# Attention and a bilinear feed-forward on one core: the second pair of heads transposed ahead of its turn, and denominators moved directly behind the weighted values

## The chip, the cores and the metric

The kernel runs on one core of a Trainium2 chip. The metric is the device time of one execution in microseconds; less is better. The core's engines are named as in the profile: PE is the matrix engine (PEld its weight loads, which can run beside its matmuls), DVE the vector engine, ACT the scalar engine, POOL the GpSimd engine, SP the engine that only issues transfers here.

## The reference

Two parts are chained. The first is attention with routing: every query and every key is given to the nearest of 16 centroids, and a query sees only the keys of its own centroid. The second is a feed-forward with two input matrices whose results are multiplied.

```python
# q, k, v: (4 batches, 8 heads, 768 positions, 64); centroids: (8, 16, 64)
q_assign = argmax(q_n @ c_n.T);  k_assign = argmax(k_n @ c_n.T)      # q_n, k_n, c_n: normalised rows
mask   = q_assign[..., :, None] == k_assign[..., None, :]
scores = where(mask, (q @ k.T) / 8, -1e9)
attn   = exp(scores - max);  attn = attn / (sum(attn) + 1e-9)
x      = (attn @ v) laid out as (3072 tokens, 512)
out    = ((x @ w_a) * (x @ w_b)) @ w_out             # w_a, w_b: 512 x 1536, w_out: 1536 x 512
```

## The kernel before

Two heads form a pair, so there are 16 pairs `p`; four pairs make a batch. The main loop counts groups `g`; six groups belong to a pair (`l` is the place in the pair), and a group is two blocks of 128 keys against 384 queries, for both heads. A group scores its own blocks (a one-hot product that carries the mask, then the product of queries and keys), and weighs the values with the exponentials of the group before. Every third group closes a half pair with its denominators: a product of a matrix of ones with the last exponentials and with a running sum `acc`. Between these lie the preparation of the next pair (`ready[l]`) and pieces of the feed-forward (`ffn`).

```python
def prep_transpose(p, i):                  # 4 of the 12 transposes of pair p, into one PSUM bank
    ps = ps_m.tile([P, 512], FP32, name="m")             # ps_m: three banks in turn
    for n in range(4):
        w, j = divmod(4 * i + n, NJ)
        nc.tensor.transpose(out=ps[:, n*P:(n+1)*P], in_=qks[p][:, w, j]..., identity=ident)
    dst = qkTs[p][:, i * 512:(i + 1) * 512]
    if p == 0 and i != 1: nc.vector.tensor_copy(out=dst, in_=ps)
    else:                 nc.scalar.copy(out=dst, in_=ps)

def prep_sim(p):    # similarity with the centroids: 4 matmuls over qkTs[p], 32 columns each
def prep_assign(ps, quarters): # five DVE steps: maximum, >=, times rank, maximum, ==
def prep_onehot_first(kq):     # pair 0: six bf16 transposes on PE, one copy on ACT, one on DVE
def keep_busy(n):   # n transposes of the identity into a bank that nobody reads

# prep_steps(p), pairs 1 to 3:
return [both(lambda: prep_transpose(p, 0), lambda: prep_transpose(p, 1)),
        both(lambda: prep_sim(p), lambda: load_v(p)),
        lambda: todo.extend(prep_assign(prep_across(p))), lambda: None,
        lambda: prep_onehot(p, 1), lambda: None]
# pairs 4 to 15: the transposes are DVE stream transposes in 32x32 blocks (across), prep_sim in step 1

# ... start of the program (cut)
first = load_first()          # q and k of pair 0: q from SP's queue, k from ACT's
centroids_in()                # norms of the centroids on DVE and ACT
order_first(*first, 0, nc.vector.tensor_copy); order_first(*first, 1, nc.scalar.copy)
# ...
keep_busy(18)
prep_transpose(0, 0); centroids_across(); prep_transpose(0, 1); prep_transpose(0, 2)
# ...
load(1); load_v(0); load_w(0); load_w(1)
prep_sim(0); keep_busy(3)
across = prep_across(0)
rest_of_first = score((0, 1))              # the q.k part of the first two blocks
keep_busy(4)
for kq in range(2):
    for step in prep_assign(across, kq): step()
    prep_onehot_first(kq)
    if kq == 0:
        keep_busy(5); rest_of_first(); keep_busy(7)
for g in range(NG + 3):
    # ...
    if 0 < g < NG: score(now)
    check_inverses()
    if 0 < g <= NG:
        for u in before: add_up(u)         # acc += exponentials, on DVE (later on POOL too)
    flush_w()
    if 0 < g <= NG: weigh(before)
    if g < NG: ready[l]()
    late = int(g > EARLY)                  # EARLY = 25
    if g % 3 == late and 0 < g - late:
        denominators(*divmod(g // 3 - 1, 2))
    # ... weights, feed-forward pieces (cut)
    if l == 0 and p + 1 < NPAIR:
        if not by_blocks(p + 1): prep_transpose(p + 1, 2)      # by_blocks: p >= 4
        load(p + 2)
```

Of the kernel before, what the change touches and what calls it, by code (L numbers as in the profile page):

```python
# [8 lines left out]
FP32 = mybir.dt.float32  # L9
# [21 lines left out]
P = 128  # L31
# [105 lines left out]
def short_path(nc, tc, ctx, c, cn, centroids_in, casts, n_far, q, k, v,  # L137
# [3 lines left out]
    B, H, S, D = q.shape  # L141
    NC = 16
    DM, DF = moe_w_a.shape
    NJ = S // P
# [6 lines left out]
    def pool(name, bufs, space=None):  # L151
        kw = {} if space is None else {"space": space}
        return ctx.enter_context(tc.tile_pool(name=name, bufs=bufs, **kw))

    zero = pool("zero", 1)
    qkp = pool("qkp", 1)
# [8 lines left out]
    hp_ = pool("hp", 2)  # L165
# [9 lines left out]
    ident, identb, ones, rank = c["ident"], c["identb"], c["ones"], c["rank"]  # L175
# [10 lines left out]
    def by_blocks(p):  # L186
        return p >= HP

    def load(p):
        if p >= NPAIR:  # L190
            return
        b, hp = divmod(p, HP)
        if by_blocks(p):
            t = qkp.tile([P, 2, S // 32, 32], FP32, name="qk")
            for w, src in enumerate((q, k)):
                for n in range(4):
                    a, d = divmod(n, 2)
                    nc.sync.dma_start(
                        out=t[32 * n:32 * n + 32, w],
                        in_=src[b, 2 * hp + a, :, 32 * d:32 * d + 32].rearrange(  # L200
                            "(j t) d -> t j d", t=32))
            qks[p] = t
            return
        t = qkp.tile([P, 2, NJ, 2, D], FP32, name="qk")
        for w, src in enumerate((q, k)):
            for a in range(2):
                nc.sync.dma_start(
                    out=t[:, w, :, a, :],
                    in_=src[b, 2 * hp + a].rearrange("(p j) d -> p j d", j=NJ))
        qks[p] = t  # L210

    def load_first():

        t = qkp.tile([P, 2, NJ, 2, D], FP32, name="qk")
        rows = hp_.tile([P, 2, 2, NJ * D], FP32, name="h")
        for eng, w, src in ((nc.sync, 0, q), (nc.scalar, 1, k)):
            eng.dma_start(out=rows[:, w], in_=src[0, 0:2].rearrange(
                "a (p j) d -> p a (j d)", j=NJ))
        qks[0] = t
        return t, rows  # L220
# [20 lines left out]
            in_=v[b, 2 * hp:2 * hp + 2].rearrange("a (p j) d -> p a (j d)", j=NJ))  # L241

    first = load_first()
    centroids_in()
    order_first(*first, 0, nc.vector.tensor_copy)
    order_first(*first, 1, nc.scalar.copy)
# [76 lines left out]
    idle = ps_o.tile([P, 512], FP32, name="O")  # L323

    def keep_busy(n):

        for _ in range(n):
            nc.tensor.transpose(out=idle[:, 0:P], in_=ident, identity=ident)
# [7 lines left out]
    def prep_transpose(p, i):  # L336
        if i == 0:
            qkTs[p] = qtp.tile([P, 2 * S], FP32, name="qkT")
        ps = ps_m.tile([P, 512], FP32, name="m")
        for n in range(4):  # L340
            w, j = divmod(4 * i + n, NJ)
            nc.tensor.transpose(  # L342
                out=ps[:, n * P:(n + 1) * P],
                in_=qks[p][:, w, j].rearrange("p a d -> p (a d)"),
                identity=ident)
        dst = qkTs[p][:, i * 512:(i + 1) * 512]
        if p == 0 and i != 1:
            nc.vector.tensor_copy(out=dst, in_=ps)
        else:
            nc.scalar.copy(out=dst, in_=ps)  # L350
# [77 lines left out]
    def prep_onehot_first(kq):  # L428

        ohTs[0] = ohT_bufs[0]  # L430
        ps = ps_m.tile([P, 1024], BF16, name="m")
        for n in (3, 4, 5, 0, 1, 2):
            w, t = divmod(n, 3)
            nc.tensor.transpose(out=ps[:, n * P:(n + 1) * P],
                                in_=oh_all[:, 4 * t + 2 * w + kq, :],
                                identity=identb)
        c0 = kq * HB
        nc.scalar.activation(out=ohTs[0][:, S + c0:S + c0 + HB],
                             in_=ps[:, HB:S], func=AF.Identity, scale=FAR,
                             bias=nfar[:, 0:1])  # L440
        nc.vector.tensor_copy(out=ohTs[0][:, c0:c0 + HB], in_=ps[:, 0:HB])  # L441
# [55 lines left out]
    def prep_steps(p):  # L497
        if p >= NPAIR:
            return [lambda: None] * 6

        def both(*fs):
            return lambda: [f() for f in fs]

        if by_blocks(p):
            steps = prep_by_blocks(p)
            ready = [lambda s=s: todo.extend(s) for s in steps]
            ready[1] = both(lambda: prep_sim(p), lambda: load_v(p), ready[1])
            return ready

        return [  # L510
            both(lambda: prep_transpose(p, 0), lambda: prep_transpose(p, 1)),
            both(lambda: prep_sim(p), lambda: load_v(p)),
            lambda: todo.extend(prep_assign(prep_across(p))),
            lambda: None,
            lambda: prep_onehot(p, 1),
            lambda: None,
        ]
# [75 lines left out]
    def denominators(p, hf):  # L593


        ps = ps_m.tile([P, 512], FP32, name="m")
        acc = accs.pop((p, hf))
        terms = [acc]
        if p < HP:
            terms.insert(0, probs[p * UPP + hf * NJ + NJ - 1])  # L600
        for n, t in enumerate(terms):
            for a in range(2):
                nc.tensor.matmul(out=ps[a * D:(a + 1) * D, 0:HB], lhsT=ones,  # L603
                                 rhs=t[:, a, :], start=(n == 0),
                                 stop=(n == len(terms) - 1))
        den = acc[:, 0, :]
        n = 4 * p + 2 * hf
        nc.scalar.activation(out=den, in_=ps[:, 0:HB], func=AF.Copy,
                             accum_out=stat[:, n:n + 1])
        den_of[p, hf] = acc  # L610
# [391 lines left out]
    NG = NPAIR * GPP  # L1002
# [13 lines left out]
    for i in range(8, len(w_parts)):  # L1016
        due.setdefault(23 + int((i - 8) / 1.5), []).append(i)

    keep_busy(18)
    prep_transpose(0, 0)  # L1020
    centroids_across()
    prep_transpose(0, 1)
    prep_transpose(0, 2)
    casts()
    for r, factor in ((slice(0, P // 2), 1.0), (slice(P // 2, P), FAR)):
        nc.vector.tensor_scalar(out=rank_far[r], in0=rank[r], scalar1=factor,
                                scalar2=None, op0=ALU.mult)
    load(1)
    load_v(0)
    load_w(0)  # L1030
    load_w(1)
# [3 lines left out]

    across = prep_across(0)
    rest_of_first = score((0, 1))
    keep_busy(4)
    for kq in range(2):
        for step in prep_assign(across, kq):  # L1040
            step()
        prep_onehot_first(kq)
        if kq == 0:
            keep_busy(5)
            rest_of_first()
            keep_busy(7)
    for g in range(NG + 3):
        p, l = divmod(g, GPP)
        if l == 0:
            ready = prep_steps(p + 1)  # L1050
        now = (2 * g, 2 * g + 1)
        before = (2 * g - 2, 2 * g - 1)
        if 0 < g < NG:
            score(now)
        check_inverses()
        if 0 < g <= NG:
            for u in before:
                add_up(u)
        flush_w()
        if 0 < g <= NG:  # L1060
            weigh(before)
        if g < NG:
            ready[l]()
        late = int(g > EARLY)
        if g % 3 == late and 0 < g - late:
            denominators(*divmod(g // 3 - 1, 2))
        parts = due.get(g, [])

        def round_next():
            if parts:  # L1070
                i = parts.pop(0)
                round_w(i)
                load_w(i + 2)

        round_next()
        if g <= EARLY:
            first, second = 4, 1
        else:
            first, second = 5, 3 if g < NG else 2
        ph = {first: (p, 0), second: (p - 1, 1)}.get(l)  # L1080
        halved = ph in den_of
        if halved:
            todo.extend(normalize(*ph))
        if ffn:
            credit += PER_GROUP[(g > 2 * BG + 3) + (g > 3 * BG + 3)]
            least = FREE_ROOM if halved and ph[1] and (ph[0] + 1) % HP == 0 else 0
            while len(ffn) > least and credit > 0:
                cost, piece = ffn.popleft()
                credit -= cost
                piece()  # L1090
                if todo:
                    todo.popleft()()
                round_next()
        else:
            credit = 0
        round_next()
        while todo:
            todo.popleft()()
        if halved:
            ffn_ready(*ph)  # L1100
        if l == 0 and p + 1 < NPAIR:
            if not by_blocks(p + 1):
                prep_transpose(p + 1, 2)
            load(p + 2)
        if l == 4 and p + 1 < NPAIR and not by_blocks(p + 1):
            prep_onehot(p + 1, 0)

    def some_ffn(n):
        for _ in range(n):
# [17 lines left out]
                     start=True, stop=True)  # L1127
# [227 lines left out]
```

## Time and profile before

The time before is 1052.72 us, the median of three runs (1052.52 to 1053.35). The profiled execution has a span of 1050.6 us.

| what | value |
|---|---|
| PE, share of the span | 99% |
| DVE / POOL / ACT, share of the span | 68% / 34% / 25% |
| granted PE clock over the span | 0.999 |
| matmuls and weight loads on PE | 7156 each |
| moved by transfers | 46.49 MB, mean 44 GB/s |
| first transposes of pair 0 begin | 5.94 us |
| group 1's scores begin | 19.03 us |

The lines are read as follows. `L342`, `L539`, `L580`, `L603`, `L358` and `L654` are the transposes of a pair, the scores, the weighted values, the denominators, the similarities with the centroids and the feed-forward's matmuls. `L438` and `L441` are the two copies of pair 0's one-hot rows, `L405` to `L409` the five steps of the assignment, `L569` the running sum of the exponentials and `L460` the DVE's stream transposes of later pairs. A line of the timeline or of a group ends with the idle time ahead of it and what ended that. A busy PE is not a PE at its peak: the ends of matmuls are modelled, and a wait can hide in a group whose time is simply longer than elsewhere.

### The profile page before, as it was taken

How to read it: one execution, taken by the hardware profiler on the slowest of the kernel's cores; microseconds unless marked ns; L12 is line 12 of the kernel's file. 1: busy time of each engine (PE TensorE's matmuls, PEld its weight loads, DVE VectorE, ACT ScalarE, POOL GpSimd, SP SyncE). 2: the span in 40 equal slices, each digit the busy share in tenths (PEclk: the TensorE clock that was granted, in tenths of full speed). 3: DMA queues.
4: the chain of work that ended last, by engine and by line, in shares of the span. 5: the costliest groups of instructions: out<-in, count | busy, mean ns of one | idle time of the engine just before them, and what ended most of it. 6: DMA issues, size and time to landing. Idle time of an engine off the chain costs nothing.

```text
span 1050.6 us, 17937 instructions
## 1 busy us (share of the span) xinstructions
PE 1036.5 (99%) x7156; PEld 510.6 (49%) x7156; DVE 709.6 (68%) x1402; ACT 260.6 (25%) x501; POOL 355.7 (34%) x329
## 2 busy tenths in 40 slices
PE   8999999999999999999999999999999999999997
PEld 5444444444445554444444555444444565444576
DVE  5778878787857548676767746767665846776752
ACT  5666333333322221212222121122121200000000
POOL 1111244555542323443545422444344310212200
PEclk9999999999999999999999999999999999999999
DMA  5334243526230130303020030300000000000001
GB/s 167 89 75 109 69 122 88 126 81 143 64 50 16 33 53 18 44 4 46 4 46 1 25 66 20 51 1 20 1 4 1 12 31 22 1 1 1 2 32 34
DMA packets 120523, 46.49 MB, mean 44 GB/s; under 512 B 106608, under 2 KB 115824, under 8 KB 120432
## 3 DMA queue, kind: packets, MB, share of 16 engines
q1 hardware_dynamic: 120016, 44.85, 18.4%
q8 instruction: 58, 0.95, 0.4%
q10 hardware_dynamic: 416, 0.43, 0.1%
q14 instruction: 33, 0.27, 0.1%
HBM read 37.78 MB, written 6.29 MB: 42 GB/s over the span
## 4 chain that ended last, share of the span: by engine, by line
PE 92%; DVE 5%; issue 1%; POOL 1%; ACT 0%; DMA 0%; DVEq 0%; POOLq 0%
PE m L654 61%; PE s L539 14%; PE O L580 12%; PE m L603 2%; PE m L358 1%; DVE raw L730 1%; PE m L342 1%; POOL xT L635 1%; DVE raw L757 0%; DVE xT L730 0%; DVE raw L874 0%; DVE ha L784 0%; DVE acc L630 0%; DVE acc L569 0%; DVE acc L623 0%
## 5 line engine op out<-in xcount | busy, mean ns | idle before, releaser
L548 ACT ACTIVATE pt<-s 128x768 f32<-128x768 f32 x192 | 145.4, 808 | 303.3 <-PE s L539 250.3
L569 POOL TENSOR_TENSOR acc<-acc,pt 128x384 f32<-128x384 f32 x144 | 152.8, 1076 | 57.9 <-ACT pt L548 41.9
L789 POOL TENSOR_TENSOR h<-h,ha 128x384 f32<-128x384 f32 x72 | 73.0, 1021 | 230.9 <-DVE ha L784 230.9
L580 PE MATMUL O<-pt,v 128*64 128x384 f32 x768 | 145.0, 499 | 0.0
L539 PE MATMUL s<-qkT 64*128 64x384 f32 x768 | 139.6, 483 | 0.0
L654 PE MATMUL m<-xT,wa_sb 128*64 128x384 f32 x672 | 119.3, 487 | 1.7 <-POOL xT L635 0.9
L654 PE MATMUL m<-xT,wb_sb 128*64 128x384 f32 x672 | 119.1, 486 | 0.0
L784 DVE TENSOR_TENSOR ha<-ha,m 128x384 f32<-128x384 f32 x126 | 66.9, 546 | 70.7 <-PE m L654 69.6
L784 DVE TENSOR_TENSOR h<-h,m 128x384 f32<-128x384 f32 x126 | 67.2, 548 | 61.1 <-PE m L654 60.4
L569 DVE TENSOR_TENSOR acc<-acc,pt 128x384 f32<-128x384 f32 x96 | 73.7, 793 | 36.0 <-POOL acc L569 35.1
L580 PEld LDWEIGHTS O<-pt,v 128*64 128x64 f32 x768 | 46.6, 136 | 86.2 <-issue 86.1
L654 PE MATMUL m<-wo_sb,h 128*64 128x256 f32 x768 | 86.7, 379 | 0.0
L539 PEld LDWEIGHTS s<-qkT 64*128 64x128 f32 x768 | 70.5, 187 | 31.4 <-issue 0.2
L635 POOL TENSOR_TENSOR xT<-xT,acc 128x384 f32<-128x384 f32 x32 | 33.0, 1033 | 143.4 <-DVE acc L630 143.4
L654 PEld LDWEIGHTS m<-xT,wa_sb 128*64 128x64 f32 x672 | 49.2, 137 | 61.3 <-issue 50.6
L654 PEld LDWEIGHTS m<-xT,wb_sb 128*64 128x64 f32 x672 | 49.2, 137 | 59.3 <-issue 55.4
L654 PE MATMUL m<-raw 128*64 128x384 f32 x384 | 70.2, 486 | 1.1 <-DVE ha L784 1.1
L654 PEld LDWEIGHTS m<-wo_sb,h 128*64 128x64 f32 x768 | 57.3, 137 | 28.3 <-issue 3.9
L654 PE MATMUL m<-xT,h 128*64 128x256 f32 x576 | 64.8, 379 | 0.1
L654 PEld LDWEIGHTS m<-xT,h 128*64 128x64 f32 x576 | 43.0, 137 | 20.9 <-issue 2.9
L654 PE MATMUL m<-xT,size 128*64 128x384 f32 x288 | 52.6, 486 | 0.0
L539 PE MATMUL s<-ohT 64*128 64x384 bf16 x384 | 48.1, 328 | 0.5 <-DVE ohT L441 0.5
(160 smaller groups left out, 1267.8 us busy)
## 6 DMA issues: line engine op xcount, KB each, us to landing
raw<-in_moe_w_a_dram SPq DMA_DIRECT2D x12, 512.0 KB, 4.2
raw<-in_moe_w_b_dram SPq DMA_DIRECT2D x12, 512.0 KB, 3.6
raw<-in_moe_w_out_dram SPq DMA_DIRECT2D x12, 512.0 KB, 3.7
qk<-in_q_dram SPq DMA_DIRECT2D x48, 96.0 KB, 3.2
qk<-in_k_dram SPq DMA_DIRECT2D x48, 96.0 KB, 3.6
v<-in_v_dram SPq DMA_DIRECT2D x24, 192.0 KB, 3.8
out_dram<-rest SPq DMA_DIRECT2D x24, 128.0 KB, 1.7
v<-in_v_dram SPq DMA_DIRECT2D x4, 384.0 KB, 4.3
```

The costliest lines, as they stand in the source:

```text
L342: nc.tensor.transpose(out=ps[:, n * P:(n + 1) * P], in_=qks[p][:, w, j].rearrange("p a d -> p (a d)"), identity=ident)
L358: nc.tensor.matmul(out=ps[32 * kq:32 * kq + 32, 0:HB], lhsT=cTb[:, hp, :], rhs=qkTs[p][:, kq * HB:(kq + 1) * HB], start=True, stop=True)
L539: nc.tensor.matmul(out=s[:, a, 0:HB], lhsT=Ts[p][r, S + j * P:S + (j + 1) * P], rhs=Ts[p][r, hf * HB:(hf + 1) * HB], start=start, stop=not ...
L548: nc.scalar.activation(out=pt, in_=s[:, :, 0:HB], func=AF.Exp, scale=SCALE)
L569: eng.tensor_tensor(out=acc[:, a, :], in0=probs[u - 1][:, a, :] if j == 1 else acc[:, a, :], in1=probs[u][:, a, :], op=ALU.add)
L580: nc.tensor.matmul(out=O_of[0][a * D:(a + 1) * D, 0:HB], lhsT=vs[p][:, a, j, :], rhs=probs[u][:, a, :], start=(j == 0), stop=(j == NJ - 1))
L603: nc.tensor.matmul(out=ps[a * D:(a + 1) * D, 0:HB], lhsT=ones, rhs=t[:, a, :], start=(n == 0), stop=(n == len(terms) - 1))
L635: nc.gpsimd.tensor_tensor(out=x, in0=x, in1=den, op=ALU.mult)
L654: nc.tensor.matmul(out=ps[half], lhsT=lhsT[:, half], rhs=rhs, start=start, stop=stop)
L730: nc.vector.tensor_tensor(out=out, in0=l, in1=r, op=ALU.subtract)
L784: nc.vector.tensor_tensor(out=out, in0=in0, in1=ps, op=op)
L789: nc.gpsimd.tensor_tensor(out=to, in0=to, in1=box[name], op=ALU.mult)
```

## The change

Pair 1's queries and keys are loaded at the start of the program, into the second buffer of the pool of `h` (which the feed-forward needs only later), and its twelve transposes are done in places where pair 0's first assignment leaves PE with nothing but idle transposes. Group 1 weighs the values of group 0 before it scores, so that PE has work while the last one-hot rows are copied. The denominators of a half pair come directly behind the weighted values, ahead of the next pair's transposes or similarities, so that work of one shape stays together and the preparation gets more time. The idle work at the start begins earlier, with matmuls on a matrix of ones that is there before the identity is.

```diff
-        t = qkp.tile([P, 2, NJ, 2, D], FP32, name="qk")
+        own, name = (hp_, "h") if p == 1 else (qkp, "qk")
+        t = own.tile([P, 2, NJ, 2, D], FP32, name=name)
...
     first = load_first()
+    load(1)
     centroids_in()
...
-        if p == 0 and i != 1:
+        if p == 0 and i != 1 or p == 1 and i == 2:
             nc.vector.tensor_copy(out=dst, in_=ps)
...
-            both(lambda: prep_transpose(p, 0), lambda: prep_transpose(p, 1)),
+            lambda: p > 1 and (prep_transpose(p, 0), prep_transpose(p, 1)),
...
-    keep_busy(18)
+    for _ in range(12):
+        nc.tensor.matmul(out=idle[0:D, 0:D], lhsT=ones, rhs=ones, start=True, stop=True)
+    keep_busy(16)
...
-    load(1)
     load_v(0)
...
     rest_of_first = score((0, 1))
-    keep_busy(4)
+    prep_transpose(1, 0)
+    keep_busy(1)
     for kq in range(2):
         for step in prep_assign(across, kq):
             step()
+        if kq == 1:
+            prep_transpose(1, 1)
+            prep_transpose(1, 2)
         prep_onehot_first(kq)
         if kq == 0:
             keep_busy(5)
             rest_of_first()
-            keep_busy(7)
...
+        if g == 1:
+            weigh(before)
         if 0 < g < NG:
             score(now)
...
-        if 0 < g <= NG:
+        if 1 < g <= NG:
             weigh(before)
-        if g < NG:
-            ready[l]()
         late = int(g > EARLY)
         if g % 3 == late and 0 < g - late:
             denominators(*divmod(g // 3 - 1, 2))
+        if g < NG:
+            ready[l]()
...
-            if not by_blocks(p + 1):
+            if p and not by_blocks(p + 1):
                 prep_transpose(p + 1, 2)
```

## The prediction

> **What bounds the kernel now.** I read the page's busy times and slices first, then the chain of waits in order of time from 0 to 120 us, then the timeline of all engines there, and last the chain from 185 to 260 us. The page says that PE is the bound:
>
> ```profile
> PE 1036.5 (99%) x7156; PEld 510.6 (49%) x7156; DVE 709.6 (68%) x1402; ACT 260.6 (25%) x501; POOL 355.7 (34%) x329
> PE   8999999999999999999999999999999999999997
> ```
>
> Only the first slice (26 us) shows PE below nine tenths. So three things can be won: the time until PE runs without a break, waits hidden inside PE's groups, and the cost of changing from one shape of matmul to another. The chain (start, duration, what) at the start:
>
> ```profile
> 17.35 0.59 ACT ohT L438
> 17.94 0.02 issue
> 17.96 0.37 DVE ohT L441
> 18.33 0.04 issue
> 18.37 0.66 PE m L342 x4
> 19.03 1.72 PE s L539 x12
> 20.75 1.44 PE O L580 x8
> 22.19 0.78 PE m L358 x8
> ...
> 29.78 1.65 PE m L603 x7
> ...
> 41.75 1.02 PE m L342 x8
> 42.77 1.44 PE m L603 x8
> 44.22 0.59 PE m L342 x4
> ...
> 93.30 1.29 PE m L603 x8
> ```
>
> Until 18.33 the chain goes through pair 0's assignment on DVE, PE and ACT; from 18.37 on it is PE alone. Denominators take 1.29 us behind weighted values (93.30), 1.44 between transposes (42.77), and 1.65 in the third group (29.78). That last one contains a wait for DVE's running sum, which the timeline shows; its bracket holds the idle time and what ended it:
>
> ```profile
> 26.65 0.56 DVE L405 TENSOR_REDUCE mx<-m 128x24 f32<-128x384 f32 x1 [1.59 <-PE m L372]
> ...
> 30.09 0.30 PEld L603 LDWEIGHTS m<-acc,ones 128*64 128x64 f32 x2 [0.34 <-DVE acc L569]
> ```
>
> The late pairs have two hidden waits. Similarities take 0.78 us where nothing holds them (22.19), but here:
>
> ```profile
> 192.44 1.23 PE m L358 x8
> ...
> 249.37 0.90 DVE qkT L460
> 250.27 0.04 issue
> 250.31 0.84 PE m L358 x4
> 251.15 0.02 issue
> 251.18 0.84 PE m L358 x4
> 252.01 0.80 PE m L603 x4
> ```
>
> PE stands for DVE's stream transposes and does the denominators, which were ready, only afterwards. In the other eight late pairs the chain has 0.78 for the similarities, without a wait.
>
> **What the Trainium skill says.** (1) "TensorEngine Tiling (Array Packing)", Key Properties: changing the tiling mode drains the engine. The trace agrees: between weighted values (128x64 tiles) and transposes (128x128) the weight loads pause 0.60 us, against 0.18 us within one shape, and a change costs about 0.15 us of PE (1.44 less 1.29). (2) "TensorE: Matmul & The Clock Gate", Part 1: PE runs at half clock until a free-running window of about 3.4 us has been busy. The trace agrees in kind: the eighteen idle transposes from 1.43 us take 3.70 us of weight loads, 0.206 us each, and at 7.84 us four take 0.42, 0.105 each. Pair 0's first four at 5.94 still take 1.13 us where four later take 0.66. (3) "DMA: Bandwidth & Descriptors", Issuing engines are not separate DMA queues, and Why small descriptors are slow: transfers of SP and ACT share the same 16 engines, and runs of 256 B are slow. Pair 1's load has 256 B runs; in the trace the DMA engines are 95% busy between 10 and 13 us, while it lands, at 214 GB/s, against peaks of 409 GB/s for pair 0's long rows.
>
> **The change part by part.**
>
> *Start, PE.* The four transposes at 18.37 (0.66 us) leave the path. The eight others of pair 1 lay at 17.15 to 18.19 beside the copies of the one-hot rows and cost nothing; in their place come eight matmul records of weighted values (1.44 us). Their inputs are there: the exponentials end at 15.35 + 1.51 = 16.86, and the values, now issued ahead of 11.37, land earlier than before. They start when the one-hot transposes end, 16.80 + 0.52 = 17.32, and end at 18.76. The one-hot rows are there by about 18.45, since ACT has one 0.59 us copy of pair 1 in front (16.86 to 17.45) and DVE follows. So the scores run 18.76 to 20.48, and the similarities begin at 20.48 instead of 22.19: 1.71 us won.
>
> *What takes a part of it back.* In the third group PE waits for the running sum. DVE starts its stretch behind the one-hot copy, about 0.1 us later than before. It had 1.59 us of idle ahead of 26.65; it would come there at 25.06 + 0.11 = 25.2, and then it has no more idle. So the sum is ready 26.65 - 25.2 = 1.45 us earlier, not 1.71, and the denominators wait about 0.3 us longer. I count 1.4 us.
>
> *Start, the fill-ins.* Four transposes and one idle one stand for four idle ones; eight stand for seven, at 0.107 us each, between 15.6 (when the bank of the similarities is read: 15.21 + 0.36) and 16.80. They fit. ACT's copy of the first four ends near 13.8, ahead of 13.95; DVE's copy of the last four (0.69 us) lies in its idle time between 16.75 and 17.96.
>
> *Start, clock and loads.* Idle work begins at about 1.05, when the ones are there (0.92 + 0.11), in place of 1.43, and runs up to about 5.7. If the clock rises before 5.94, the first four transposes give 1.13 - 0.66 = 0.47 us; if not, nothing. Against that, pair 1's load is behind q on SP's queue and beside k on ACT's. k took 4.2 us to land, at 5.46; ACT's copy ends at 6.40 and is needed at about 7.1, so a delay up to 0.7 us is free. I let the two cancel: 0.
>
> *Pairs 2 and 3.* Before: 1.02 + 1.44 + 0.59 = 3.05 us. After: denominators 1.29 and twelve transposes in a row, 1.02 + 4 x 0.107 = 1.45, so 2.74. Two times 0.31 is 0.6 us. The running sum ended at 39.25, long ahead of 41.7.
>
> *Late pairs.* With 0.65 us of denominators in front (the chain has 0.65 where they follow weighted values), both halves of the stream transposes are done in time: 192.44 + 0.65 is past 192.77, and 250.23 + 0.65 = 250.88 for a half done at 250.27, the second at about 251.3 for one done at 251.12. That gives 1.23 - 0.78 = 0.45 and 252.01 - (250.23 + 0.78) = 1.00, together 1.45 us. In the other eight the order of the same shapes changes and the number of changes of shape does not: 0.
>
> Sum: 1.4 + 0.6 + 1.45 = 3.45 us, 0.33%: 1052.72 - 3.45 = 1049.3 us.
>
> **The rivals.** *DVE takes over.* In the stretches 188 to 200 and 245 to 258 us DVE is busy 10.72 of 12 and 11.74 of 13 us; what PE wins there it could lose at the next product of the feed-forward. For it: DVE is 90% busy. Against it: at 197.16 and 255.51 DVE itself waits 1.01 us for PE. If it holds for all of the late gain, the time is 1050.8. *The early load delays pair 0.* If 256 B runs push k back by over 0.7 us, each further tenth is lost at the start; with 1.5 us of delay the time is about 1050.1. Against it: q stands in front of the new load on the same queue, and in the trace the DMA engines are through with q and k by 5.0 us (0.83 busy from 3.5 to 5.0, nothing from 5 to 8), so less than 2 us of k's transfer can overlap with it. *All of the start's gain is caught by the third group's wait.* If DVE were no earlier there than before, only the later gains would be left: 1050.7. Against it: the 1.59 us that DVE idles for PE. *The clock rises earlier*: 1048.8.
>
> **Range and chances.** The sum is 3.45 us. The terms for the late pairs and the start are read off waits that vanish, and can only be smaller; clock and load can add or take half a microsecond; three runs of before spread over 0.83 us. So 1048.3 to 1051.0 should hold it 8 times in 10. All of it lies far inside 2% (21 us): chances 0.01 faster, 0.98 within 2%, 0.01 slower.
>
> **What would show it.** In the profile after: similarities of pair 1 begin near 20.5 us and PE has no transposes behind the one-hot copy; the denominators of the third group take about 1.9 us, as their wait grows; those of groups 6 and 12 take 1.29 and are followed by twelve transposes; no similarities of over 0.85 us stay near 190 and 250 us. I am wrong if pair 0's first transposes come after 5.94, if k's copy moves the similarities of pair 0 past 8.63, or if a wait of PE for DVE appears behind 192 or 250 us that was not there.

## The result and the profile after

The changed kernel takes **1049.05 us** (median of six runs, 1048.40 to 1049.59), the kernel before 1052.62 us (six runs, 1052.16 to 1053.35): a ratio of **0.9965 [0.9952, 0.9978]**. The profiled executions have spans of 1047.3 and 1050.6 us, so 3.3 us between the two traces have to be found. The predicted time was 1049.3 us.

First the page of the changed kernel (busy us, share, instructions):

```profile
PE 1034.4 (99%) x7168; PEld 510.2 (49%) x7168; DVE 711.2 (68%) x1403; ACT 259.8 (25%) x500; POOL 355.1 (34%) x329
```

PE has twelve more matmul records and still 2.1 us less of busy time: much of what was won had been counted as busy, as waits inside groups. In the page's slices PE's first digit is now 9 (before 8).

The chain of waits of the changed kernel (start, duration, what). Line numbers are three higher than before: `L345`, `L361`, `L542`, `L583`, `L606`, `L657` are the transposes, similarities, scores, weighted values, denominators and feed-forward matmuls, and `L437` the transposes of the one-hot rows.

```profile
16.79 0.51 PE m L437 x6
17.30 1.44 PE O L583 x8
18.74 1.72 PE s L542 x12
20.46 0.78 PE m L361 x8
21.24 1.82 PE s L542 x12
...
28.14 1.65 PE m L606 x7
...
40.12 1.29 PE m L606 x8
41.41 1.46 PE m L345 x12
...
190.23 0.65 PE m L606 x4
190.87 0.78 PE m L361 x8
...
247.54 0.65 PE m L606 x4
248.19 1.16 PE m L361 x8
```

Up to 16.79 the chain still passes through pair 0's assignment; then PE runs on with weighted values where ACT's and DVE's copies and four transposes stood. The similarities of pair 1 begin 1.73 us earlier than before (20.46 for 22.19). Pair 2 has 1.29 + 1.46 = 2.75 us in place of 3.05. Both late waits are shorter, but the second one, at 248.19, is not gone: 1.16 us where 0.78 is the time without a wait.

The timeline of the changed kernel (start, busy time, what; in brackets the idle time ahead of it and what ended that) shows the places where it could have gone otherwise:

```profile
1.08 2.64 PEld L1023 LDWEIGHTS O<-ones 128*64 128x64 f32 x24 [1.08 <-DVE ones L80]
3.59 0.22 DVE L94 TENSOR_TENSOR wo_sb<-wo_sb 128x64 f32<-128x64 f32 x1 [2.56 <-DMA wo_sb<-in_centroids_dram]
3.83 2.32 PEld L331 LDWEIGHTS O<-ident 128*128 128x128 f32 x16
6.38 0.42 PEld L345 LDWEIGHTS m<-ident,qk 128*128 128x128 f32 x4 [0.22 <-DVE nfar L305]
...
25.02 0.56 DVE L408 TENSOR_REDUCE mx<-m 128x24 f32<-128x384 f32 x1
...
28.46 0.30 PEld L606 LDWEIGHTS m<-acc,ones 128*64 128x64 f32 x2 [0.34 <-DVE acc L572]
...
248.12 0.14 PEld L361 LDWEIGHTS m<-qkT,cTb 128*32 128x32 f32 x4 [0.60 <-PE O L583]
...
248.51 0.14 PEld L361 LDWEIGHTS m<-qkT,cTb 128*32 128x32 f32 x4 [0.25 <-DVE qkT L463]
```

Four readings. The first DVE step on the centroids (`L94`) starts at 3.59 instead of 3.16, and pair 0's first transposes at 6.38 instead of 5.94; but they take 0.66 us in the chain instead of 1.13, since the clock is up by then, so the similarities of pair 0 begin at 8.61 (before 8.63). DVE reaches the maximum (`L408`) at 25.02 without an idle time, 1.63 us earlier than before. The third group's denominators have the same wait of 0.34 us for the running sum. And the first four matmuls of the late similarities wait for nothing from DVE; the other four stand 0.39 us later, behind the second stream transpose.

| place | before | after | won, us |
|---|---|---|---|
| end of group 3's denominators | 31.43 | 29.79 | 1.64 |
| denominators and transposes, pairs 2 and 3 | 3.05 each | 2.75 each | 0.60 |
| similarities and denominators near 190 us | 1.23 + 0.80 | 0.65 + 0.78, and 0.15 more in the piece behind | 0.45 |
| from scores to scores near 250 us | 10.93 | 10.28 | 0.65 |
| from the scores near 255 us to the end of the span | 792.6 | 792.6 | 0.0 |

The sum is 3.3 us, as the spans have it.

### The profile page after: what moved, and what is told of

Read it like the earlier page. It is cut to its first block, busy times and chain, and to the rows that moved or that the text cites. A ratio compares the mean times of both kernels' runs of the same rounds, so it can differ in the third digit from the quotient of the medians.

```text
span 1047.3 us, 17963 instructions
## 1 busy us (share of the span) xinstructions
PE 1034.4 (99%) x7168; PEld 510.2 (49%) x7168; DVE 711.2 (68%) x1403; ACT 259.8 (25%) x500; POOL 355.1 (34%) x329
## 4 chain that ended last, share of the span: by engine, by line
PE 93%; DVE 4%; issue 1%; POOL 1%; ACT 0%; DVEq 0%; POOLq 0%
PE m L657 61%; PE s L542 15%; PE O L583 12%; PE m L606 2%; PE m L361 1%; DVE raw L733 1%; POOL xT L638 1%; PE m L345 0%; DVE raw L760 0%; DVE xT L733 0%; DVE raw L877 0%; DVE ha L787 0%; DVE acc L633 0%; DVE acc L572 0%; PE O L1023 0%
## 5 line engine op out<-in xcount | busy, mean ns | idle before, releaser
L583 PE MATMUL O<-pt,v 128*64 128x384 f32 x768 | 145.0, 499 | 0.0
L542 PE MATMUL s<-qkT 64*128 64x384 f32 x768 | 139.7, 482 | 0.0
L657 PE MATMUL m<-xT,wa_sb 128*64 128x384 f32 x672 | 119.3, 487 | 1.7 <-POOL xT L638 0.9
L657 PE MATMUL m<-xT,wb_sb 128*64 128x384 f32 x672 | 119.2, 487 | 0.0
L583 PEld LDWEIGHTS O<-pt,v 128*64 128x64 f32 x768 | 46.6, 136 | 85.8 <-issue 85.6
L657 PE MATMUL m<-wo_sb,h 128*64 128x256 f32 x768 | 86.8, 379 | 0.0
L542 PEld LDWEIGHTS s<-qkT 64*128 64x128 f32 x768 | 70.5, 187 | 31.3 <-issue 0.2
L657 PEld LDWEIGHTS m<-xT,wa_sb 128*64 128x64 f32 x672 | 49.3, 137 | 61.3 <-issue 51.0
L657 PEld LDWEIGHTS m<-xT,wb_sb 128*64 128x64 f32 x672 | 49.0, 137 | 60.1 <-issue 54.3
L657 PE MATMUL m<-raw 128*64 128x384 f32 x384 | 70.3, 487 | 1.1 <-DVE ha L787 1.1
L657 PEld LDWEIGHTS m<-wo_sb,h 128*64 128x64 f32 x768 | 57.0, 137 | 29.0 <-issue 3.8
L657 PE MATMUL m<-xT,h 128*64 128x256 f32 x576 | 64.8, 379 | 0.1
L657 PEld LDWEIGHTS m<-xT,h 128*64 128x64 f32 x576 | 43.0, 137 | 21.0 <-issue 2.9
L657 PE MATMUL m<-xT,size 128*64 128x384 f32 x288 | 52.6, 486 | 0.0
L542 PE MATMUL s<-ohT 64*128 64x384 bf16 x384 | 48.2, 328 | 0.5 <-DVE ohT L444 0.5
```

The source lines that it names most:

```text
L542: nc.tensor.matmul(out=s[:, a, 0:HB], lhsT=Ts[p][r, S + j * P:S + (j + 1) * P], rhs=Ts[p][r, hf * HB:(hf + 1) * HB], start=start, stop=not ...
L583: nc.tensor.matmul(out=O_of[0][a * D:(a + 1) * D, 0:HB], lhsT=vs[p][:, a, j, :], rhs=probs[u][:, a, :], start=(j == 0), stop=(j == NJ - 1))
L657: nc.tensor.matmul(out=ps[half], lhsT=lhsT[:, half], rhs=rhs, start=start, stop=stop)
```

## The experiments

The theory to be tested: the gain consists of two parts that don't need each other, the start (pair 1's transposes in gaps and group 1's weighing ahead of its scores) and the order of denominators and preparation; what is missing of it is a second half of similarities that comes late. The rivals: the early load and the idle work account for part of the result or take some of it back; the gain of the start comes from another step than the one named; the missing part near 250 us is only due to the earlier arrival of PE. Experiments are compared with the kernel before on the same chip: 1051.80 us for the first four (the first chip), 1053.11 for the next four (the second chip), 1051.79 for the last four (the first chip again). Which chip the comparison above ran on is not known. Where the start is compared between traces, times are counted from the similarities of pair 0, since the landing of the first loads moves all of it.

**The start alone.** The changed kernel with the old order:

```diff
-        late = int(g > EARLY)
-        if g % 3 == late and 0 < g - late:
-            denominators(*divmod(g // 3 - 1, 2))
         if g < NG:
             ready[l]()
+        late = int(g > EARLY)
+        if g % 3 == late and 0 < g - late:
+            denominators(*divmod(g // 3 - 1, 2))
```

> The changed kernel with the old order of denominators and preparation: only the start is changed. Theory (the gains are separate and add up): the start gives 1.64 us of span at the third group's denominators and nothing later gives it back, so the span is near 1049.0 and the time near 1051.0; pairs 2 and 3 show 3.05 us for transposes, denominators, transposes again, and the similarities near 191 and 248 us take 1.23 and twice 0.84 us again. Rival (the order pays only because the start was changed, or the reverse): the time is within 0.5 us of the changed kernel or of the kernel before.

Measured: 1050.70 us, ratio 0.9990 [0.9982, 0.9999], span 1048.3. From pair 0's similarities to the denominators of group 3 it takes 27.52 - 7.99 = 19.53 us, as in the changed kernel (28.14 - 8.61), against 29.78 - 8.63 = 21.15 before: the start brings 1.62 us without the new order. In the medians it is only 1.10 us: the profiled run is the lowest of twelve, which lie between 1049.99 and 1051.36. The kernels with fewer idle transposes, below, show where the rest may go. Its chain of waits has the old late wait whole, 0.84 + 0.84 us from 248.09. Though PE is here 2.2 us earlier than before (scores at 244.81 for 247.04), the two halves still cost what they did. From scores to scores it is 10.93 us (244.81 to 255.74), as before: the start neither loses nor wins anything later.

**The order alone.** The kernel before with the reverse of that edit.

> The kernel before with only the new order: denominators ahead of the preparation. Theory: 0.60 us for pairs 2 and 3, 0.45 near 192 us and 0.65 near 250 us, together 1.7 us: time near 1050.9, and the similarities near 250 us still take 1.16 us, because the second half of the DVE's transposes is late against PE by the same amount whatever the start does. Rival (the 0.35 us missing near 250 us come from the shifted start): the similarities near 250 us take 0.78 us here and the gain is 2.05 us.

Measured: 1050.12 us, ratio 0.9984 [0.9978, 0.9991], span 1048.3. Pair 2 has 1.29 + 1.46 = 2.75 us, the similarities near 190 us 0.78; those near 250 us take 1.36 us. The timeline of this kernel:

```profile
247.84 1.83 DVE L460 STREAM_TRANSPOSE qkT<-qk 128x768 f32<-128x768 f32 x2
...
249.13 0.14 PEld L358 LDWEIGHTS m<-qkT,cTb 128*32 128x32 f32 x4 [0.60 <-PE O L580]
...
249.72 0.14 PEld L358 LDWEIGHTS m<-qkT,cTb 128*32 128x32 f32 x4 [0.45 <-DVE qkT L460]
```

DVE's two transposes end at 249.67 and the second half starts at once, 0.59 us behind the first; 1.36 is 0.58 more than 0.78. The expected 1.16 was too low, since DVE's transposes begin 2.44 us behind the scores here (247.84 for 245.40) and 2.24 in the changed kernel; what shifts them was not tried. So the shortfall exists without the new start, and the rival that only the earlier arrival causes it falls. On this chip the parts add up: 1.1 us for the start and 1.7 for the order, against 2.6 and 2.8 for the next two kernels, which have both.

**Group 1 weighs behind its scores again.** The changed kernel without that one move:

```diff
-        if g == 1:
-            weigh(before)
...
-        if 1 < g <= NG:
+        if 0 < g <= NG:
             weigh(before)
```

> The changed kernel with group 1 weighing the values behind its scores, as before. Theory (of the start's 1.7 us, 0.66 comes from the transposes that left the path and the rest from the weighted values that fill the time until the one-hot rows are there): scores begin at about 18.4 us, similarities of pair 1 at about 21.5 in place of 20.46, and the time is 1.0 us above the changed kernel, near 1050.1. Rival (DVE's chain of pair 1 sets the third group's denominators anyway): the loss is gone by the third group and the time is the changed kernel's within 0.3 us.

Measured: 1049.17 us, ratio 0.9977 [0.9968, 0.9985], span 1047.8. The expectation was wrong. From pair 0's similarities to group 3's denominators it is 28.14 - 8.13 = 20.01 us: weighing early is worth 20.01 - 19.53 = 0.48 us, and the transposes' leaving 21.15 - 20.01 = 1.14. The chain of this kernel shows why:

```profile
16.86 0.59 ACT ohT L441
...
17.49 1.63 PE s L542 x10
```

Before, PE began at 18.37 with four transposes, behind DVE's copy of the one-hot rows, 0.43 us after the end of ACT's copy. Here it begins with scores right behind ACT's copy, while DVE's runs from 17.47 to 17.83: the transposes had waited for DVE's copy, which empties the bank that they write next (three are used in turn), and these scores don't. So what leaves the path is 0.66 us of transposes and 0.43 us of waiting, 1.09 of the 1.14. Weighing early then wins 0.58 us at the similarities of pair 1 (20.56 - 8.13 less 20.46 - 8.61) and gives back 0.10 in the scores behind them, 1.82 us for 1.72.

**The load of pair 1 held back**, to after a step of POOL:

```diff
         t = own.tile([P, 2, NJ, 2, D], FP32, name=name)
+        if p == 1:
+            nc.gpsimd.memset(t[:, 0, 0, 0, 0:1], 0.0)
...
     first = load_first()
-    load(1)
     centroids_in()
...
     nc.gpsimd.memset(oh_all, 0.0)
+    load(1)
```

> The changed kernel with pair 1's load held back to about 3 us by a small memset on POOL behind the clearing of the one-hot buffer. Theory (the early load delays the centroids' landing, from 3.1 to 3.6 us, and with it the whole chain of their norms): the first step on the centroids starts at 3.16 us again, pair 0's first transposes at about 5.95 and still take 0.66 us, its similarities start at about 8.2, and the time is 0.4 us below the changed kernel, near 1048.6. Rival (the centroids landed late by chance, or for another reason): the first step stays at 3.5 to 3.6 us and the time is the changed kernel's. Second rival (k is pushed back instead): the similarities stay at 8.6.

Measured: 1048.98 us (1048.18 to 1049.82), ratio 0.9974 [0.9963, 0.9984], span 1046.5. The first step on the centroids starts at 3.00, but in the start-only kernel and in the one before this, with the early load, at 2.91 and 3.11: on this chip there is no delay that the load could cause. Inconclusive by itself.

**The changed kernel again**, unaltered, on the second chip:

> The changed kernel unaltered, as the measure for the runs beside it. In the earlier runs the first step on the centroids started at 2.9 to 3.6 us with the early load and at 3.0 to 3.2 without it. Theory (the 3.6 us of the first profile were chance): it starts near 3.0 here. Rival (the early load costs it half a microsecond): 3.5 or later. Time 1049.1 or somewhat less, 3.0 to 3.6 us below the kernel before.

Measured: 1048.84 us (1048.70 to 1049.22), ratio 0.9963 [0.9949, 0.9976], span 1047.0. Centroids at 3.52, pair 0's first transposes at 6.30, its similarities at 8.53: the picture of the first profile. That is the rival's sign, but no kernel without the early load was profiled on this chip, so load and chip cannot be told apart here.

**Idle work without the matmuls on ones.**

```diff
-    for _ in range(12):
-        nc.tensor.matmul(out=idle[0:D, 0:D], lhsT=ones, rhs=ones, start=True, stop=True)
-    keep_busy(16)
+    keep_busy(18)
```

> The changed kernel with eighteen idle transposes in place of twelve matmuls on the ones and sixteen transposes. Theory[...]: the idle transposes stay near 0.206 us each up to 5.1 us; the rise comes somewhere between 4.8 and 7 us, and the time is 0 to 0.5 us above the changed kernel. Rival (transposes do not raise the clock, matmuls do): pair 0's first transposes are slow in any case, 1.1 us and more, and the time is at least 0.5 us above.

Measured: 1049.00 us (1048.74 to 1049.22), ratio 0.9963 [0.9949, 0.9976]: no difference from the changed kernel. Its timeline:

```profile
1.43 3.70 PEld L331 LDWEIGHTS O<-ident 128*128 128x128 f32 x18 [1.43 <-POOL ident masks.py:199]
...
6.55 0.42 PEld L345 LDWEIGHTS m<-ident,qk 128*128 128x128 f32 x4 [1.43 <-DVE nfar L305]
```

Eighteen transposes at 0.206 us each run slow to their end at 5.13, no weights are loaded for 1.43 us, and pair 0's first four take 0.42 us of loads, the fast rate. The matmuls on ones bring nothing that was measured here. In this profile the clock rose between 5.13 and 6.55 us with nothing but transposes on PE before it; no run leaves the idle work out, so how far the clock depends on it is not shown. "TensorE: Matmul & The Clock Gate" of the Trainium skill, Part 4, says that a transpose doesn't count as busy work for the clock in the same way; for these transposes of 32-bit data the measurement differs, and it decides.

**The last assignment step later.** The five DVE steps of pairs 1 to 3 are issued in one group and stand ahead of the running sum. Here the fifth comes a group later:

```diff
+        last = []
...
-            lambda: todo.extend(prep_assign(prep_across(p))),
-            lambda: None,
+            lambda: (last.extend(prep_assign(prep_across(p))), todo.extend(last[:4])),
+            lambda: todo.append(last[4]),
```

> The changed kernel with the fifth step of the assignment of pairs 1 to 3 issued one group later, behind the running sum. Theory (the denominators of the groups 3, 9 and 15 wait for the sum because DVE works off the assignment first): their time falls from 1.65 to 1.29 us, 0.36 in each of three places, 1.1 us in all, and the one-hot transposes are no later. Rival (the sum waits for the exponentials on ACT): they keep 1.6 us and the time is the changed kernel's.

Measured: 1047.79 us (1047.75 to 1047.88), ratio 0.9952 [0.9939, 0.9966], 1.05 us below the changed kernel on this chip. The denominators of the groups 3 and 15 in the chain of this kernel (group 9 has 1.29 as well):

```profile
28.18 1.29 PE m L608 x8
...
78.42 1.29 PE m L608 x8
```

Each had 1.65 us (the last 1.66), so 3 x 0.36 = 1.08 us were a hidden wait for the running sum. The prediction had seen the first and counted it as something that only grows; it can be removed.

**And the late similarities behind a piece of the feed-forward.** The kernel just described, in which the late pairs' similarities are held until the first piece is done:

```diff
-        if g < NG:
+        held = g > EARLY and l == 1
+        if g < NG and not held:
             ready[l]()
...
                 piece()
+                if held and g < NG:
+                    ready[l]()
+                held = False
```

> The kernel of the run before this with, in addition, the similarities of the late pairs moved behind the first piece of the feed-forward. Theory (near 248 us the second half of the similarities starts late and cannot run beside the first): they take 0.78 us there in place of 1.16, 0.4 us less than the run before, 1.5 us less than the changed kernel. Rival (PE then waits for DVE at the next product instead): the 0.4 us appear in the feed-forward's matmuls that follow.

Measured: 1047.27 us (1047.12 to 1047.71), ratio 0.9947 [0.9934, 0.9961]. The chain of this kernel near 250 us:

```profile
247.77 2.58 PE m L659 x16
250.35 0.78 PE m L361 x8
```

With 2.58 us of feed-forward in front, the similarities take 0.78. From scores to scores it is 9.90 us (243.96 to 253.86) against 10.27 in the kernel without this edit: 0.37 us, which is the wait of 0.38, and no new one behind it. In this profile the clock rose late, which the next kernels take up.

**The same kernel again, on the first chip.**

> The kernel with the assignment's last step later and the similarities behind the first piece, unaltered, beside the two runs with less idle work. Theory: its time is within 0.6 us above theirs, and its first transposes start when the idle work ends (up to 7.0 us) or when q is copied (5.7 to 6.5 us), whichever is later.

Measured: 1047.72 us, ratio 0.9958 [0.9944, 0.9972], but five runs between 1046.61 and 1048.10. The timeline of the one profiled:

```profile
3.84 3.16 PEld L331 LDWEIGHTS O<-ident 128*128 128x128 f32 x16
...
6.96 0.47 PEld L345 LDWEIGHTS m<-ident,qk 128*128 128x128 f32 x4
```

Pair 0's first transposes have no wait behind their name: they stand right behind the idle ones, which ran slowly almost to their end. Their inputs were there earlier; in the next kernel, on the same chip with the centroids 0.2 us later, they begin at 5.93.

**Half of the idle transposes:** `keep_busy(8)` for `keep_busy(16)`, the rest as in the kernel just shown.

> The last kernel (assignment's last step later, similarities behind the first piece) with eight idle transposes behind the matmuls on the ones in place of sixteen. In that kernel's profile the clock rose late, the idle work lasted to 7.0 us, and pair 0's first transposes stood behind it. Theory: twelve matmuls of 0.22 us and eight transposes of at most 0.206 us end by 5.4 us, so pair 0's transposes never wait for idle work; the time is the last kernel's or up to 0.6 us less, by where the clock rises. Rival (without so much idle work the clock rises later, and the transposes are slow): the first four take 1.1 us and the time is 0.4 us more.

Measured: **1046.67 us** (1046.61 to 1046.73), ratio 0.9951 [0.9937, 0.9966], the fastest of all but for the kernel after this, which is level with it. Its timeline:

```profile
3.83 1.24 PEld L331 LDWEIGHTS O<-ident 128*128 128x128 f32 x8
...
5.93 0.42 PEld L345 LDWEIGHTS m<-ident,qk 128*128 128x128 f32 x4 [0.86 <-DVE nfar L305]
```

The loads of the idle work end 0.86 us before the data are there, the clock is up all the same (0.42 us), and the five runs lie within 0.12 us instead of 1.49. Pair 0's similarities begin at 8.16 here and at 9.24 in the kernel with sixteen, and the two spans, 1045.0 and 1046.1 us, differ by the same 1.1 us. Its median is 1.05 us below that of the kernel with sixteen, on the same chip; the lowest run of that one, 1046.61, is what eight give nearly every time. Against before it is 5.1 us, against the variants of the changed kernel on this chip (1048.98, 1049.17) over 2 us.

**The load held back in that kernel** (the edit of the held load on top):

> The run before with pair 1's load held back by the memset on POOL. On the second chip the first step on the centroids started at 3.5 to 3.8 us in all four kernels with the early load; with the load held, or without it, it was 3.0 to 3.2, but on other chips. Theory (the load delays the centroids by half a microsecond): 3.0 to 3.2 us here, against 3.5 and more in the run before, and 0.4 us less time. Rival (it differs between chips and executions whatever is loaded): the start is within 0.2 us of the run before, and so is the time.

Measured: 1046.70 us (1046.62 to 1046.99), ratio 0.9952 [0.9938, 0.9966]; centroids at 3.22 against 3.15. Holding the load changes nothing on this chip.

**The kernel before, profiled again** on the first chip:

> The kernel before once more, for its start on the same chip: both theories of the centroids differ here as in the run before (3.0 to 3.2 us without an early load, or what the chip gives every kernel). Similarities near 250 us take twice 0.84 us again, or up to 0.2 us more or less, as DVE's place against PE varies.

Measured: 1051.64 us, span 1049.9. Centroids at 3.07; pair 0's first transposes at 5.85 already at the fast rate (0.43 us of loads), similarities of pair 0 at 8.10. So the slow 0.71 us that the profile of before showed is not there in every execution of it. The late waits are: 0.84 + 0.84 + 0.80 from 249.79.

## Why the prediction was right, point by point

**Start, PE: right in place, its cause half right.** Predicted: group 1's scores at 18.76 and similarities at 20.48; measured 18.74 and 20.46. That the absolute times agree so well is luck, since it needs the 0.43 us lost and the 0.47 us won ahead of them, below. And the account was read as transposes worth 0.66 us and the rest from weighing early. With weighing put back, the first is 1.14 us and the second 0.48. What was overlooked is that the transposes at 18.37, not the scores, waited for DVE's copy.

**What takes a part of it back: mis-sized, 1.4 for a measured 1.64.** The step that failed is "DVE starts its stretch behind the one-hot copy, about 0.1 us later than before", with the maximum at "25.2" and denominators that "wait about 0.3 us longer". The copy came at 17.95 as before, since ACT's copy of pair 1 in front of it ran from 16.73 to 17.33 and so was done when the one-hot transposes were; the maximum came at 25.02, and the denominators have 1.65 us in both kernels. A small loss that the prediction did not have stands beside it: the second group's scores take 1.82 for 1.72, since they now wait for ACT's exponentials (0.10 us).

**Start, fill-ins: right.** No transpose of pair 1 appears in the chain between 16.79 and 20.46.

**Start, clock and loads: 0 is what came out, by luck and not for the reasons given.** The clock did rise in time (0.66 for 1.13, so 0.47 us won), and the centroids, not k, came 0.43 us later. The size of the idle work was wrong: ending at "about 5.7" left 1.35 us for twelve matmuls on ones, behind which sixteen transposes need 3.3; they took 2.64, 0.22 each, and it ended at 6.15 only because the clock rose at about 5.1. On the first chip the term was not 0. The start is worth 1.10 us there in the medians, for 1.62 in its trace, and with half the idle transposes the kernel with both later edits falls by 1.05 us: the change's own idle work takes back a part of what the start wins. Whether the early load delays the centroids stays open for the chips where they came late (3.5 to 3.8 in the four variants profiled on the second chip): the kernel before was not profiled there. On the first chip it doesn't.

**Pairs 2 and 3: right.** Predicted 2.74 each, measured 2.75, in the order-only kernel too.

**Late pairs: 0.45 right, 1.00 wrong, measured 0.65.** The step that failed is "the second at about 251.3 for one done at 251.12". It took the two halves for parts that follow one another, the second due about 0.4 us after the first. The four blocks of 32 columns run beside each other, so 0.78 us is the time of both halves together, and a delay of the second half counts in full. The trace of before shows it too: a half alone takes 0.84 us there (250.31), both together 0.78 (22.19). Four traces agree, to within 0.06 us:

| kernel | loads of the second half after the first, us | similarities, us | over 0.78 |
|---|---|---|---|
| before | 0.86 | 1.70 | 0.92 |
| the changed one | 0.39 | 1.16 | 0.38 |
| the order alone | 0.59 | 1.36 | 0.58 |
| weighing put back | 0.80 | 1.61 | 0.83 |

"TensorEngine Tiling (Array Packing)" of the Trainium skill, Key Properties, says that different tiles can execute loads and matmuls in parallel; the table agrees, and with that sentence applied to these matmuls most of the wait could have been read from the trace before: the loads of the second half stood at 251.17, 0.36 us after those of the first would have come with the denominators in front (about 250.81, 0.07 ahead of the chain's 250.88). The other eight late pairs: 0, as predicted; behind 255 us the two traces take the same 792.6 us.

**The rivals.** DVE took nothing back: the feed-forward pieces behind the similarities have 5.31 us in both places, and the last row of the first table is 0. The third group's wait did not grow at all. The two mis-sized terms, 0.24 too low and 0.35 too high, nearly cancel: that 3.45 predicted meets 3.3 in the spans is partly luck. The medians differ by 3.57 us in the first comparison, by 4.27 on the second chip, and by 2.6 and 2.8 on the first for the two close variants of the changed kernel; part of that is a kernel before that starts better there (pair 0's similarities at 8.10 instead of 8.63 in its second profile). Why before is slower on the second chip was not tried.

**Its own signs.** Three of them came out otherwise. Pair 0's first transposes came at 6.38, after the 5.94 that was to mean being wrong; the faster clock made it good. The third group's denominators took 1.65 us for "about 1.9". And 1.16 us of similarities stayed near 250 us, where none of over 0.85 was to stay. New waits of PE for DVE behind 192 or 250 us did not appear, and pair 0's similarities stayed at 8.61.

## What to carry to other kernels

When matmuls of several column tiles run side by side, ask for the last operand, not for the first: half of it late by 0.4 us costs 0.4 us. Before crediting a filler with a gain, put it back alone: here the larger part came from what no longer waited in front of it. And idle work for the clock has a right length: end it before the first data arrive, since work queued behind it waits for a rate that it may not have.

## What the runs showed of the hardware

- The clock rose between at most 2.8 and about 5.8 us after the beginning of idle work. This is worked out from the mean of the idle loads, 0.206 us each when slow and 0.107 when fast: in the changed kernel sixteen loads in 2.32 us are about six slow and ten fast ones, so the clock rose at 3.83 + 1.27 = 5.1. In ten profiles with the idle matmuls from 1.08 us it was up by 3.84 in one (the last assignment step later, sixteen loads in 1.73 us), rose between 4.1 and 5.1 in seven, and near 6.9 in two. "TensorE: Matmul & The Clock Gate", Part 1, calls the window free-running, so that the number of slow matmuls varies; these runs agree that it varies, but by more than the 0.5 us to either side that the part gives.
- On the first chip the four kernels with sixteen idle transposes behind the matmuls on ones spread over 1.37 to 1.64 us, the four others over 0.12 to 0.63. That the rise of the clock makes the difference is inferred from the profiled runs; the others have no profile.
- A slow idle matmul of 64 columns cost 0.22 us (2.64 / 12, two loads each), no less than a slow transpose of 128 (0.206).
- The centroids' first use was at 2.9 to 3.2 us in every profile on the first chip and at 3.5 to 3.8 on the second, and one kernel that was profiled on both had 2.96 and 3.55. It is a difference between chips or executions that is as large as most of the terms in this prediction.
